# Moving row loads and the stores of the first q from SyncE's DMA queue to GpSimd's in a transformer block

## The chip, the cores and the metric

The kernel runs on one core of one Trainium2 chip. The metric is device time in microseconds (us) for one execution. A run gives several executions of a kernel, with the kernel before run in the same rounds on the same chip.

Engine names are those of the profile: PE is TensorE (matmuls), PEld its weight loads, DVE VectorE, ACT ScalarE, POOL GpSimd, SP SyncE, which here only issues DMAs. SPq is SyncE's sequencer. Of the DMA queues in the profiles, q1 carries what SyncE issues, q0 what GpSimd issues (22.02 MB in the kernel before, the sum of its transfers) and q10 what ScalarE issues. The profile gives the time of each queue's packets as a share of the core's 16 DMA engines; the shares of a stretch can add up to over 100% (108.1% from 16 to 25 us in the kernel before).

## The reference

One transformer block over 2,048 rows of 1,024 numbers in bfloat16: a layer norm, q, k and v products, a dilated attention over 8 positions at distance 2, an output product, a second layer norm, and a gated product with 3,584 columns.

```python
h = x + _A_ref(_layernorm(x, axis=-1), A_wqkv, A_wo)     # qkv, attention, output product
h2 = h + _B_ref(_layernorm(h, axis=-1), B_w_gate, B_w_up, B_w_down)
return h2
```

Only the first layer norm, the qkv product and the loads that attention needs are touched by the change.

## The kernel before

The rows are worked on in four chunks of 512 (c = 0 to 3), each of four tiles of 128 rows (t = 0 to 3). The qkv product wants normalised rows with the 1,024 columns on the partitions. For chunk 0 TensorE turns them itself; for the later ones a DMA transpose does:

```python
def transpose(self, t):                      # Norm1, one row tile of chunk c; line 225
    ...
    nc.sync.dma_start_transpose(lnTs[c][:, :, bass.ts(t, 128)], self.lns[t][:])

def load_x(c, what, eng):                    # four loads of 256 KB; line 198
    tiles = []
    for t in range(4):
        xt = hp.tile([128, D], BF, tag="h", name=f"{what}{c}_{t}")
        eng.dma_start(xt[:], x[bass.ds(c * TC + t * 128, 128), :])
        tiles.append(xt)
    return tiles
```

The product makes six blocks of 512 columns for a chunk (0 and 1 are q, 2 and 3 k, 4 and 5 v), each of four groups m of eight matmuls. ScalarE casts each group, and a DMA stores it to DRAM, from where GpSimd loads it again in the layout that attention wants (qD, kD, vD). The load of q waits until the stores of q have landed.

```python
def evac_qkv(c, m, ps):
    sg = t1k.tile([128, HB + TC], BF, tag="t1k", name=f"sg{c}_{m}")
    nc.scalar.copy(sg[:, HB:HB + TC], ps[:])
    ...
    if m < 8:                                # q: 128 KB, line 297
        nc.sync.dma_start(qd[c][...]...)
        return
    ...                                      # k, v: 144 KB, line 303
    nc.sync.dma_start(dst[...]..., win)

def load_qk(c):
    ...
    nc.gpsimd.dma_start(qD[:], qd[c].rearrange("c g d s -> (c g) d s"))   # 1 MB, line 399
    nc.gpsimd.dma_start(kD[:], kd[c].rearrange("c g d s -> (c g) d s"))
```

The schedule of the first 60 us. `pump(n)` issues the 1 MB weight blocks w1, w2, ... of the product from SyncE. `bg` holds background work (statistics, normalisation, transposes, attention) that is placed between groups of the product.

```python
pump(2, w1)
xtiles[1] = load_x(1, "x", nc.sync)
pump(4)                                      # w2, w3
xtiles[2] = load_x(2, "x", nc.sync)
...
bg.add(rows_gen(norm1[1], True))             # chunk 1: statistics, normalise, transpose
rows2 = rows_gen(norm1[2], False)            # chunk 2: the same, not transposed yet
bg.add(rows2)
...
qkv(0, range(1, 4))                          # chunk 0, blocks 1 to 3
load_qk(0)
bg.finish(rows2)
for t in range(4):
    norm1[2].transpose(t)
xtiles[3] = load_x(3, "x", nc.sync)
...
qkv(1, range(4))                             # chunk 1 needs all four of its transposes
```

Of the kernel before, what the change touches and what calls it, by code (L numbers as in the profile page):

```python
# [23 lines left out]
HB = 16  # L24
TC = 512
# [52 lines left out]
def kernel(  # L78
# [11 lines left out]
    nc = tc.nc  # L90
    x = A_x.flatten_outer_dims()
# [23 lines left out]
    qd = [dram.tile([4, H, DH, SUB], BF, name=f"qd{c}") for c in range(NCH)]  # L115
# [4 lines left out]
    bg = Background()  # L120
# [36 lines left out]
    def pump(limit=None, wt=None):  # L157
        state["limit"] = limit or state["limit"]
        while state["next"] < state["limit"] and state["live"] < 7:
            key, src, n = stream[state["next"]]  # L160
            if wt is None:
                wt = wpool.tile([128, KO, 512], BF, tag="w", name="w_" + "_".join(map(str, key)))
            nc.sync.dma_start(wt[:, 0:n, :], src)
            wts[key] = wt
            wt = None
            state["next"] += 1
            state["live"] += 1

    def retire(n=1):
        state["live"] -= n  # L170
        pump()
# [22 lines left out]
    def load_x(c, what, eng):  # L194
# [6 lines that stand above are left out]
# [3 lines left out]
    xtiles = {}  # L204
# [33 lines left out]
    def stats_gen(n):  # L238
        for t in range(4):
            n.stat(t)  # L240
            yield 1.5
# [46 lines left out]
# [3 lines that stand above are left out]
        hg = m % 8  # L291
        if m >= 8:
            nc.scalar.copy(sg[:, 0:HB], halo[:, m - 8, :])
            if c + 1 < NCH:
                nc.scalar.copy(halo[:, m - 8, :], ps[:, TC - HB:TC])
        if m < 8:
            nc.sync.dma_start(qd[c][:, 4 * hg:4 * hg + 4, :, :].rearrange("c g d s -> (g d) c s"),
                              sg[:, HB:HB + TC].rearrange("p (c s) -> p c s", c=4))
            return
        dst = (kd, vd)[m // 8 - 1][c]  # L300
        base = sg[:, 0:1]
        win = bass.AP(base.tensor, base.offset, [list(base.ap[0]), [SUB, 4], [1, SUB + HB]])
        nc.sync.dma_start(dst[:, 4 * hg:4 * hg + 4, :, :].rearrange("c g d s -> (g d) c s"), win)
# [61 lines left out]
    pump(2, w1)  # L365
    xtiles[1] = load_x(1, "x", nc.sync)
    pump(4)
    xtiles[2] = load_x(2, "x", nc.sync)
    norm1 = {c: Norm1(c) for c in (1, 2, 3)}
    bg.add(rows_gen(norm1[1], True))  # L370
    rows2 = rows_gen(norm1[2], False)
# [1 line left out]
    for j in range(4):  # L373
        evac_qkv(0, j, ps0[j])
    bg.now = 17.0

    def mm_group(ps, wt, j, rhs):
        for ko in range(KO):
            nc.tensor.matmul(ps[:], lhsT=wt[:, ko, bass.ts(j, 128)], rhs=rhs[:, ko, :],  # L379
                             start=(ko == 0), stop=(ko == KO - 1))  # L380

    def qkv(c, blocks, last=False):
        for b in blocks:
            for j in range(4):
                ps = psum.tile([128, TC], F32, tag="mm", name=f"ps{c}_{b}_{j}")
                mm_group(ps, wts["qkv", b], j, lnTs[c])
                evac_qkv(c, b * 4 + j, ps)
                bg.step(GROUP_US)
            if last:
                retire()  # L390
# [5 lines left out]
    def load_qk(c):  # L396
        qD = att.tile([128, DH, SUB], BF, tag="qD", name=f"qD{c}")
        kD = att.tile([128, DH, SUB + HB], BF, tag="kD", name=f"kD{c}")
        nc.gpsimd.dma_start(qD[:], qd[c].rearrange("c g d s -> (c g) d s"))
        nc.gpsimd.dma_start(kD[:], kd[c].rearrange("c g d s -> (c g) d s"))  # L400
        qkv_in["q", c], qkv_in["k", c] = qD, kD
# [250 lines left out]
    def start_attention(c):  # L652
        stored.add(c)
        atts[c] = attention(c)
        bg.add(atts[c], bg.now + (16.0 if c == 0 else 0.0))

    qkv(0, range(1, 4))
    load_qk(0)
    bg.finish(rows2)
    for t in range(4):  # L660
        norm1[2].transpose(t)
    xtiles[3] = load_x(3, "x", nc.sync)
    pump(6)
    bg.add(stats_gen(norm1[3]), bg.now + 6.0)
    start_attention(0)
    qkv(1, range(4))
    qkv(0, range(4, 6))
# [88 lines left out]
```

## Time and profile before

| | before |
|---|---|
| time, median of 3 executions (range) | 809.99 us (809.59 to 810.6) |
| TensorE busy | 794.0 of 808.9 us |
| TensorE waits for chunk 1's transposed rows | 4.3 us |
| granted clock after that pause | 0.51, for 6.0 us |
| chunk 1's product starts at | 42.48 us |

How to read it: TensorE is nearly always busy, so what counts is its few pauses, and the slow clock that a pause may bring (here 0.51 after the pause of 4.3 us). Below, T1 to T4 are the four transposes of chunk 1, in order.

### The profile page before, as it was taken

To read this page: it belongs to the slowest core of one execution; us is meant where nothing else is said; L and a number is where in the kernel's file an instruction comes from. 1 tells how busy PE (TensorE), PEld (TensorE's weight loads), DVE (VectorE), ACT (ScalarE), POOL (GpSimd) and SP (SyncE) were. 2 spreads that over 40 slices of the span, in tenths; PEclk is the share of its full clock that TensorE was granted. 3 is DMA by queue.
4 is the path that set the end of the run, shared out by engine and by line. 5 is a ranking of instruction groups with operands and counts; after the bars stand their busy time and mean duration, and the time that the engine had idled before them with its cause. 6 is when DMAs were issued, how large, how long until landed. Compare 5 with 4: busy or idle time off the path is not lost.

```text
span 808.9 us, 9878 instructions
## 1 busy us (share of the span) xinstructions
PE 794.0 (98%) x3700; PEld 410.3 (51%) x3769; DVE 552.1 (68%) x580; ACT 254.3 (31%) x562; POOL 165.3 (20%) x160
## 2 busy tenths in 40 slices
PE   8889999999999999999999999999999999999998
PEld 5334444444444444444444444466666666644445
DVE  6519999999899998998989926645646556311111
ACT  4516445323333321013333100244555555400000
POOL 0000000200002000010000010597867778000000
PEclk9989999999999999999999999999999999999999
DMA  7998693897956869667637596542313233466500
GB/s 261 249 268 201 167 269 88 265 288 197 330 172 214 286 243 213 213 216 239 202 105 237 172 245 178 130 121 62 104 53 105 68 90 98 158 208 191 179 27 27
DMA packets 195200, 144.32 MB, mean 178 GB/s; under 512 B 83408, under 2 KB 187984, under 8 KB 193104
## 3 DMA queue, kind: packets, MB, share of 16 engines
q1 hardware_dynamic: 191568, 121.66, 53.7%
q0 software_dynamic: 3584, 22.02, 8.3%
q8 instruction: 30, 0.49, 0.3%
q14 instruction: 18, 0.15, 0.1%
HBM read 114.29 MB, written 22.02 MB: 169 GB/s over the span
## 4 chain that ended last, share of the span: by engine, by line
PE 89%; DVE 7%; DMA 2%; issue 1%; ACT 0%; SPq 0%; DVEq 0%
PE ps L379 18%; PE acc L558 15%; PE pg L379 12%; PE pu L379 12%; PE wo L500 7%; PE pz L609 6%; PE py L609 6%; PE px L609 6%; PE pv L609 3%; PE accl L548 3%; DVE pv L462 2%; DMA lnT<-ln 1%; DVE pv L470 1%; PE ps L341 1%; DVE oD L472 1%
## 5 line engine op out<-in xcount | busy, mean ns | idle before, releaser
L379 PE MATMUL ps<-lnT,w_qkv 128*128 128x512 bf16 x721 | 161.3, 383 | 5.2 <-DMA lnT<-ln 4.3
L379 PEld LDWEIGHTS <-w_qkv 128*128 128x128 bf16 x736 | 72.6, 99 | 93.3 <-issue 8.6
L379 PE MATMUL pg<-lnT,w_wg 128*128 128x512 bf16 x439 | 105.0, 379 | 0.5
L379 PE MATMUL pu<-lnT,w_wu 128*128 128x512 bf16 x439 | 104.9, 379 | 0.4
L558 PE MATMUL acc<-w_wd,gs 128*128 128x512 bf16 x439 | 96.7, 379 | 0.5
L540 DVE TENSOR_TENSOR h<-acc,h 128x512 bf16<-128x512 f32 x28 | 17.4, 682 | 91.1 <-PE acc L558 91.1
L290 ACT CAST sg<-ps 128x512 bf16<-128x512 f32 x96 | 55.0, 587 | 68.9 <-PE ps L379 65.4
L462 DVE TENSOR_TENSOR pv<-vD,at 128x4096 bf16<-128x4096 bf16 x32 | 72.5, 2286 | 0.3
L419 DVE TENSOR_TENSOR prod<-qD,kD 128x4096 bf16<-128x4096 bf16 x32 | 72.3, 2283 | 0.1
L379 PEld LDWEIGHTS <-w_wu 128*128 128x128 bf16 x448 | 43.8, 98 | 52.9
L558 PEld LDWEIGHTS <-gs 128*128 128x128 bf16 x448 | 43.8, 98 | 52.9
L379 PEld LDWEIGHTS <-w_wg 128*128 128x128 bf16 x448 | 43.8, 98 | 52.9
L525 ACT CAST gs<-pg 128x512 bf16<-128x512 f32 x56 | 32.9, 588 | 100.0 <-PE pg L379 96.6
L500 PE MATMUL wo<-w_wo,oT 128*128 128x512 bf16 x251 | 55.6, 379 | 0.3
L474 POOL DMA_DIRECT2D od<-oD x4 | 2.2, 542 | 253.1 <-DVE oD L472 253.1
L609 PE MATMUL px<-lnT,w_pair 128*128 128x512 bf16 x210 | 52.5, 380 | 1.0
L585 POOL TENSOR_TENSOR sw<-w_pair 128x512 fp32r<-128x512 bf16 x28 | 36.5, 1304 | 75.6 <-DMA w_pair<-in_B_w_gate_dram 43.3
L530 ACT CAST us<-pu 128x512 bf16<-128x512 f32 x56 | 32.8, 587 | 57.5 <-PE pu L379 54.1
L500 PEld LDWEIGHTS <-oT 128*128 128x128 bf16 x256 | 25.1, 98 | 30.2
L181 ACT ACTIVATE rs<-mv,eps 128x1 f32<-128x1 f32 x32 | 9.5, 296 | 95.5 <-DVE mv L178 91.9
L587 POOL TENSOR_TENSOR sw<-w_pair 128x512 fp32r<-128x512 bf16 x28 | 36.9, 1319 | 0.0
L421 DVE TENSOR_TENSOR prod<-prod 128x4096 bf16<-128x4096 bf16 x16 | 36.6, 2288 | 0.3
(127 smaller groups left out, 1057.9 us busy)
## 6 DMA issues: line engine op xcount, KB each, us to landing
w_wd<-in_B_w_down_dram SPq DMA_DIRECT2D x32, 896.0 KB, 6.3
w_wg<-in_B_w_gate_dram SPq DMA_DIRECT2D x14, 1024.0 KB, 7.1
w_wu<-in_B_w_up_dram SPq DMA_DIRECT2D x14, 1024.0 KB, 5.5
w_wo<-in_A_wo_dram SPq DMA_DIRECT2D x8, 1024.0 KB, 8.0
w_pair<-in_B_w_gate_dram SPq DMA_DIRECT2D x14, 512.0 KB, 4.0
w_pair<-in_B_w_up_dram SPq DMA_DIRECT2D x14, 512.0 KB, 5.3
w_qkv<-in_A_wqkv_dram SPq DMA_DIRECT2D x5, 1024.0 KB, 10.9
kd<-sg SPq DMA_DIRECT2D x32, 144.0 KB, 3.1
```

Of the source, the lines that this page charges most:

```text
L290: nc.scalar.copy(sg[:, HB:HB + TC], ps[:])
L379: nc.tensor.matmul(ps[:], lhsT=wt[:, ko, bass.ts(j, 128)], rhs=rhs[:, ko, :], start=(ko == 0), stop=(ko == KO - 1))
L419: nc.vector.tensor_tensor(prod[:, j], qD[:], kD[:, :, o:o + SUB], ALU.mult)
L421: nc.vector.tensor_tensor(prod[:, :, 0:16], prod[:, :, 0:16], prod[:, :, 16:32], ALU.add)
L462: nc.vector.tensor_tensor(pv[:, j], vD[:, :, o:o + SUB], at[:, w, None, :].to_broadcast((128, DH, SUB)), ALU.mult)
L500: nc.tensor.matmul(ps[:], lhsT=oTs[c][:, kk, t, :], rhs=wts["wo", c, hf][:, kk, :], start=(kk == 0), stop=(kk == KO - 1))
L525: nc.scalar.copy(gs[:], pg[:])
L530: nc.scalar.copy(us[:], pu[:])
L558: nc.tensor.matmul(acc[t][:], lhsT=hT[f][:, bass.ts(t, 128)], rhs=wts["wd", c, hf, b][:, j, :], start=(f == 0), stop=(f == NF - 1))
L585: nc.gpsimd.tensor_tensor(sw[:, 0], a21, a22, ALU.add)
L587: nc.gpsimd.tensor_tensor(sw[:, 2], a11, a21, ALU.subtract)
L609: nc.tensor.matmul(ps[:], lhsT=lhs[:, ko, :], rhs=rhs[:, ko, :], start=(fresh and ko == 0), stop=(ko == 3), skip_group_check=not fresh)
```

## The change

The intent: in the order in which SyncE issues its DMAs, the first transpose of chunk 1 stands behind the four row loads of chunk 2 (5.85 us from 14.62) and six stores of q (7.54 us from 20.57), so it is issued at 28.20. If row loads and q stores go through GpSimd's queue, the transposes are issued earlier, and TensorE should not wait for them.

```diff
@@ evac_qkv
         if m < 8:
-            nc.sync.dma_start(qd[c][...]...)
+            (nc.gpsimd if c == 0 else nc.sync).dma_start(qd[c][...]...)
@@
     pump(4)
-    xtiles[2] = load_x(2, "x", nc.sync)
+    xtiles[2] = load_x(2, "x", nc.gpsimd)
@@
-    qkv(0, range(1, 4))
+    qkv(0, range(1, 2))
+    xtiles[3] = load_x(3, "x", nc.gpsimd)
+    qkv(0, range(2, 4))
     load_qk(0)
     bg.finish(rows2)
     for t in range(4):
         norm1[2].transpose(t)
-    xtiles[3] = load_x(3, "x", nc.sync)
     pump(6)
-    bg.add(stats_gen(norm1[3]), bg.now + 6.0)
+    bg.add(stats_gen(norm1[3]))
```

It has three parts: the rows of chunk 2 on GpSimd's queue ("x2"), the q stores of chunk 0 on it ("q stores"), and the rows of chunk 3 on it and earlier ("x3").

More of the change, by code (lines that the diff above doesn't have):

```diff
@@ L296, in evac_qkv @@
         if m < 8:
-            nc.sync.dma_start(qd[c][:, 4 * hg:4 * hg + 4, :, :].rearrange("c g d s -> (g d) c s"),
-                              sg[:, HB:HB + TC].rearrange("p (c s) -> p c s", c=4))
+            (nc.gpsimd if c == 0 else nc.sync).dma_start(qd[c][:, 4 * hg:4 * hg + 4, :, :].rearrange("c g d s -> (g d) c s"),
+                sg[:, HB:HB + TC].rearrange("p (c s) -> p c s", c=4))
             return
```

## The prediction

The forecast came to 806.5 us: 1.0 us won by an earlier start of chunk 1 and 2.9 us of half clock make 3.9 us, and 3.5 after the chance of one in seven. That the clock stays full in the pauses that are left was the author's estimate, as the trace before has one long pause there (4.3 us, then a clock of 0.51). That three of four x2 tiles go ahead of w1 (the 2.1 us) was an estimate too. The 0.216 us of a matmul is that of the chain of waits (1.73 us for 8). The 1.2 us of a transpose are an estimate: its 256 KB at the 205 GB/s that the kernel before moved from 28 to 34 us would take 1.3 us.

> **What bounds the kernel now.** I read the page first, then TensorE's waits, the chain of waits, stretches around the one long wait, and last the DMA queues there.
>
> ```profile
> PE 794.0 (98%) x3700; PEld 410.3 (51%) x3769; DVE 552.1 (68%) x580; ACT 254.3 (31%) x562; POOL 165.3 (20%) x160
> ...
> PE ps L379 <- DMA lnT<-ln: 4.3, 1, 4.3
> PE warm_ps L284 <- DVE warm L270: 1.2, 1, 1.2
> PE ps L341 <- DMA w_qkv<-in_A_wqkv_dram: 1.1, 1, 1.1
> ```
>
> TensorE is busy for 794.0 of 808.9 us, so all its idle time is 14.9 us. Only one wait is in reach of this change: the 4.3 us in which the qkv product of chunk 1 (line 379) waits for the transposed rows lnT. The other two are start-up, before any instruction that is moved. What that wait costs is more than 4.3 us:
>
> ```profile
> 31.00:38.00 7.00, 7.00 (x34) 3.07 (x32) 4.44 (x9) 3.66 (x15) 0.70 (x1) 1.00 1.16 186
> 38.00:42.40 4.40, 0.22 (x2) 0.00 (x0) 0.04 (x1) 1.13 (x6) 0.00 (x0) 0.90 0.81 259
> 42.40:48.40 6.00, 5.70 (x14) 2.08 (x16) 0.51 (x1) 0.59 (x1) 0.00 (x1) 0.51 1.33 205
> 48.40:54.00 5.60, 5.60 (x28) 2.53 (x27) 0.00 (x0) 1.76 (x3) 0.54 (x1) 1.00 0.98 265
> ```
>
> Columns: stretch, length, busy time (instructions) of TensorE, its weight loads, VectorE, ScalarE and GpSimd, granted clock, DMA share, GB/s. After the pause the granted clock is 0.51 for 6.0 us: 14 matmuls there, against 28 in the 5.6 us after it. At the later rate (0.20 us each by this count; 6.65 us for 30, so 0.22, by the chain below) those 14 would take 3.0 us, so the slow clock costs about 2.9 us. The wait is worth 4.3 + 2.9 = 7.2 us, 0.9% of 810. That is the most the change can win; nothing else on TensorE waits for what it moves.
>
> Why is lnT late? The chain:
>
> ```profile
> 17.77 6.65 PE ps L379 x30
> 28.20 3.17 DMA lnT<-ln
> 34.18 8.05 DMA lnT<-ln
> 42.23 0.25 issue
> 42.48 2.29 PE ps L379 x5
> ```
>
> The first transpose is issued at 28.20 and lands in 3.17 us; the fourth is issued at 34.18 and needs 8.05. So there are two delays: a late issue, and a slow landing. The issue, from the timeline, then the two DMA queues from 36.5 to 41.5 (packets, MB, share of the 16 engines):
>
> ```profile
> 14.62 5.85 SPq L198 DMA_DIRECT2D x<-in_A_x_dram  x4
> 20.57 7.54 SPq L297 DMA_DIRECT2D qd<-sg  x6
> 28.20 1.35 SPq L225 DMA_TRANSPOSE lnT<-ln  x1
> 34.44 0.70 POOL L399 DMA_DIRECT2D qD<-qd  x1 [24.38 <-DMA qd<-sg]
> ...
> q0 software_dynamic: 128, 1.04, 91.5%
> q1 hardware_dynamic: 418, 0.10, 12.3%
> ```
>
> SyncE is held up 5.85 us by the four rows of chunk 2 and 7.54 us by six q stores. The first normalised row was ready at 20.9 (normalisation at 20.37, 0.55 us), so its transpose is 7.3 us late. GpSimd's 1 MB load of q (qD) then starts 0.26 us after the fourth transpose and takes 91.5% of the engines. Alone, that transpose would have landed at 34.18 + 3.2 = 37.4, before TensorE ran dry at 38.2. The collision makes the wait; the late issue makes the collision possible.
>
> [...] From 51 to 54 us [...] 107 packets of q0 beside 87 of q1, but 0.99 MB against 0.02, because GpSimd's packets are 8 to 9 KB and SyncE's 256 B. [...] The DMA share from 16 to 25 us is already 108.1%, all q1: there is none to spare.
>
> **The change part by part.** The instruction order shows that TensorE's and VectorE's orders stay as they are and ScalarE moves three casts; SyncE loses 16 DMAs (4 of x2, 8 of qd, 4 of x3) and GpSimd gains them. Bytes are equal.
>
> Removed: SyncE's 5.85 us and 13 us of stores ahead of transposes. They can be issued at about 21, 23, 25 and 27; the third now stands behind the first k store, which waits for the first product of block 2.
>
> Moved, and now in the way: GpSimd's queue works beside the weights. TensorE needs w1 at 17.28, then, at 32 matmuls of 0.216 us (6.9 us) a block, w2 at 24.2 and w3 at 31.1. In the trace w1, issued at 10.09, lands 5.0 later (15.1), w2 9.3 after 12.69 (22.0), w3 11.9 after 13.17 (25.0). Margins: 2.2, 2.2, 6.1 us.
> - x2: 1 MB at some 360 GB/s (rate of 16 to 25 us) is 2.9 us. Issued from 10.1 on as x0's tiles come free[...]. About three of four tiles precede w1: 15.1 + 2.1 = 17.2. No wait, or 0.5 us.
> - q stores: eight of 128 KB. SyncE's landed 0.45 us apart, taken as the cost of each (estimate). Six have passed by the time w2 lands: 22.0 + 2.9 + 6 x 0.4 = 27.3 against 24.2 needed (24.7 if w1 was late). A new wait of 2.0 to 3.0 us.
> - x3, from about 26: another 2.9 us. w3: 25.0 + 2.9 + 3.2 + 2.9 = 34.0, needed at 27 + 6.9 = 33.9. A wait of 0 to 1 us, longer if qD, now issued near 29, overtakes it.
> - Transposes: behind w3 in the same queue, each about 1.2 us of the engines, sharing with qD's 1 MB: last at 39 to 42. TensorE would finish block 3 at 27 + 13.8 = 40.8. A wait of 0 to 1 us.
>
> Sum: chunk 1 starts near 41.5 instead of 42.48 (1.0 us won), and [...] the 2.9 us of half clock go too: 3.9 us. With a one in seven chance that a pause still trips the clock, 3.5 us. 809.99 - 3.5 = 806.5.
>
> Beside other work: attention of chunk 0 on VectorE may start earlier, as x3's statistics no longer wait 14.3 us for rows loaded at 50.2. Later VectorE waits are not TensorE's waits, so this is worth nothing in the total.
>
> **The rivals.** *A: clean win.* The SyncE queue is what matters, GpSimd's data comes late or trickles, the weights keep their margins, and all 7.2 us go: about 803. For it: transposes could be issued 7 us sooner, and margins of 2.2 us exist. Against it: a DMA share of 108% in that stretch; 1 MB plus stores must displace something[...]. *B: the wait moves to the weights.* w2 waits 3.5 us or more[...], and w3 or the transposes wait again behind x3 and qD: chunk 1 starts at 43 to 46, about 809 to 813. For it: the slow start of qD in the trace (1.04 MB in 5 us, and only 0.10 MB beside it). Against it: w3 has 6 us of margin, and a late block 2 pushes its need back. *C: nothing.* The fourth transpose just meets qD again, both earlier: 809 to 810. My number lies between A and B.
>
> **Range and chances.** The clean win bounds it below at 802.8. Above, a w2 wait of 4 us with cold clock and one more small wait give 811. 802.5 to 811 should hold it 8 times in 10. Two per cent is 16.2 us; the win cannot exceed 7.2, and a loss of 16 would take four waits like the one removed. So within 2% 0.98, faster 0.005, slower 0.015.
>
> **What would show it.** TensorE's waits: no 4.3 us on lnT; instead a wait on w_qkv near 24 us of 2 to 3 us. The granted clock near 1.00 from 38 to 54. First transpose issued near 21 to 22, not 28. The landing of w2 at 11 us or more after its issue, not 9.3; w3 15 or more, not 11.9. Granted clock below 1 after 24 means rival B; no wait over 0.5 us anywhere in 17 to 60 means rival A, and my stores and rows got less of the engines than I gave them. A new wait beyond 60 us, on a row tile or a q, would show that I missed a dependency.

## The result, and the profile after

The kernel after took 820.86 us (median of 4, 820.48 to 822.8), against 809.79 us (808.6 to 810.6) for the kernel before in the same rounds. The ratio is 1.0143, with a 95% interval of 1.0122 to 1.0163. A ratio here is the mean time of one kernel's runs over that of the other's of the same rounds, so it is not quite the ratio of the medians quoted. The change is slower, by less than 2%; the time lies 9.9 us above the predicted range.

First the engines' busy time in the profile of the kernel after (span 819.0 us, before 808.9). TensorE's count shows that all 3,769 matmuls are recorded, while 69 were missing before, so busy times of the two aren't compared; waits and times of day are.

```profile
PE 799.4 (98%) x3769; PEld 410.6 (50%) x3769; DVE 553.3 (68%) x580; ACT 255.5 (31%) x562; POOL 175.5 (21%) x176
```

TensorE's waits after (line, what it waited for: us in total, times, longest):

```profile
PE ps L379 <- DMA lnT<-ln: 11.7, 1, 11.7
PE ps L379 <- DMA w_qkv<-in_A_wqkv_dram: 2.1, 1, 2.1
```

The wait that was to go has grown from 4.3 to 11.7 us, and the new wait for w2 is there with 2.1 us. Now stretches around the two (same columns as in the prediction):

```profile
24.20:26.40 2.20, 0.06 (x2) 0.02 (x2) 1.85 (x5) 0.98 (x3) 1.24 (x2) 0.99 1.04 355
26.40:41.90 15.50, 15.50 (x64) 6.54 (x64) 4.45 (x10) 4.62 (x18) 2.20 (x5) 0.89 1.35 173
41.90:53.60 11.70, 0.12 (x1) 0.00 (x0) 2.49 (x5) 3.53 (x14) 0.00 (x0) 0.71 0.91 131
53.60:57.00 3.40, 3.33 (x8) 1.16 (x9) 3.22 (x7) 0.00 (x0) 0.00 (x0) 0.50 1.38 223
57.00:63.00 6.00, 6.00 (x29) 2.76 (x28) 2.80 (x7) 3.88 (x12) 0.53 (x1) 1.00 1.19 217
```

The clock fell twice: to half for 3.4 us after each pause (the first is inside the second line, whose mean is 0.89 for that reason). In the second stretch the 8 matmuls took 3.33 us; at the 6.00 us for 29 of the line after it they would have taken 1.7 us. So 3.4 us at half clock cost 1.7 us, twice that 3.4 us. So the ledger: after, 2.1 + 11.7 + 3.4 = 17.2 us; before, 4.3 + 2.9 = 7.2 us. The difference of 10.0 us is the difference of the spans (10.1 us), so nothing after 60 us matters.

Why the transposes are late, from the chain of waits after:

```profile
25.34 0.80 DVE ln L186
26.14 0.54 DVE st L177
26.68 26.90 DMA lnT<-ln x2
53.58 0.09 issue
53.67 6.35 PE ps L379 x21
```

and from the timeline of SyncE's and GpSimd's issues (start, length of the group, what, how many; in brackets the idle time before it and what ended it):

```profile
21.36 8.82 SPq L225 DMA_TRANSPOSE lnT<-ln  x2
30.68 0.38 SPq L303 DMA_DIRECT2D kd<-sg  x1
31.16 14.81 SPq L225 DMA_TRANSPOSE lnT<-ln  x2
...
25.90 2.15 POOL L198 DMA_DIRECT2D x<-in_A_x_dram  x4
34.41 0.54 POOL L399 DMA_DIRECT2D qD<-qd  x1 [6.35 <-DMA qd<-sg]
```

The early issue worked for T1, which is issued at 21.36 instead of 28.20. It did not for T4, which is issued at 40.75 instead of 34.18 although its row was ready at 26.1: SyncE needed 9.5 us to issue T3 alone (31.16 to 40.66), where a transpose took it 1.3 us before. And the landing takes the whole gain and more:

| | T1 | T2 | T3 | T4 |
|---|---|---|---|---|
| issued | 21.36 | 26.68 | 31.16 | 40.75 |
| landed | 37.35 | 42.88 | 52.85 | 53.58 |
| us | 16.0 | 16.2 | 21.7 | 12.8 |

Before, T1 landed in 3.17 us. These times run from issue to landing, so they hold what stood ahead in SyncE's own queue: w3 for T1, and the earlier transposes for the others. The weights do not explain the lateness, though: w3 landed at 30.1, and T1 7.2 us after it. From then on only two things are left in flight: transposes (with k stores) in SyncE's queue, and in GpSimd's the last q stores (landed by 33.85), the rows of chunk 3 (landed 35.9 to 40.7), then qD (issued 34.41, landed 52.67). These never leave a gap. The DMA view of 28 to 40 us (packets, MB, rate; then packets, MB and share of the 16 engines of each queue):

```profile
DMA packets 1903, 1.71 MB, mean 143 GB/s; under 512 B 1563, under 2 KB 1583, under 8 KB 1901
...
q0 software_dynamic: 414, 1.31, 70.5%
q1 hardware_dynamic: 1488, 0.39, 31.4%
```

This is the riddle that the experiments are for. The sum of what was to be moved is no more than predicted, but the engines moved it at 143 GB/s, where the prediction had taken some 360 GB/s from the stretch before. They look busy, because packets took long, and carried little: by these shares 0.33 us for one of 3.2 KB in q0 and 0.04 us for one of 0.26 KB in q1, against 0.18 us for 4.3 KB and 0.02 us for 0.27 KB with plain copies in place of the transposes (e8_plain, below).

### The profile page after: what moved, and what is told of

The parts are those of the page before. It is cut to its first block, busy times and chain, and to the rows that moved or that the text cites. A ratio compares the mean times of both kernels' runs of the same rounds, so it can differ in the third digit from the quotient of the medians.

```text
span 819.0 us, 9960 instructions
## 1 busy us (share of the span) xinstructions
PE 799.4 (98%) x3769; PEld 410.6 (50%) x3769; DVE 553.3 (68%) x580; ACT 255.5 (31%) x562; POOL 175.5 (21%) x176
## 4 chain that ended last, share of the span: by engine, by line
PE 95%; DMA 4%; DVE 0%; SPq 0%; ACT 0%; issue 0%
PE acc L558 21%; PE ps L379 18%; PE pg L379 12%; PE pu L379 12%; PE wo L500 7%; PE pz L609 6%; PE py L609 6%; PE px L609 6%; DMA lnT<-ln 3%; PE pv L609 3%; PE accl L548 3%; PE ps L341 1%; DMA w_qkv<-in_A_wqkv_dram 1%; PE pt L331 0%; SPq L257 0%; DVE ln L186 0%
## 5 line engine op out<-in xcount | busy, mean ns | idle before, releaser
L379 PE MATMUL ps<-lnT,w_qkv 128*128 128x512 bf16 x736 | 162.8, 384 | 13.8 <-DMA lnT<-ln 11.7
L609 PE MATMUL px<-lnT,w_pair 128*128 128x512 bf16 x224 | 55.6, 381 | 0.0
## 6 DMA issues: line engine op xcount, KB each, us to landing
w_qkv<-in_A_wqkv_dram SPq DMA_DIRECT2D x5, 1024.0 KB, 12.8
```

The source lines that it names most:

```text
L379: nc.tensor.matmul(ps[:], lhsT=wt[:, ko, bass.ts(j, 128)], rhs=rhs[:, ko, :], start=(ko == 0), stop=(ko == KO - 1))
L609: nc.tensor.matmul(ps[:], lhsT=lhs[:, ko, :], rhs=rhs[:, ko, :], start=(fresh and ko == 0), stop=(ko == 3), skip_group_check=not fresh)
```

## The experiments

Two theories to start with. **Bytes**: the engines carry so many bytes a microsecond (362 GB/s was measured from 16 to 25 us in the kernel before) whatever is in flight, and what is late is late because of what is ahead of it. **Collision**: transposes in flight beside another queue's transfers slow both down, beyond their bytes. The first set tries the parts one by one, the second asks what is needed for the slowing, the third builds on what was learned, and the last tries to give it a size. Times are medians. `n` is the number of runs of the kernel tried.

| kernel | time, us | before, same rounds | ratio (95%) | n |
|---|---|---|---|---|
| e1_x2_only | 813.18 | 810.56 | 1.0044 (1.0014 to 1.0075) | 4 |
| e2_qd_only | 806.32 | 810.56 | 0.9954 (0.9922 to 0.9985) | 4 |
| e3_x3_only | 813.29 | 810.56 | 1.0039 (1.0013 to 1.0065) | 4 |
| e4_without_x3 | 807.00 | 810.56 | 0.9960 (0.9929 to 0.9992) | 4 |
| e5_before_gate | 809.89 | 810.27 | 1.0003 (0.9982 to 1.0023) | 6 |
| e6_gate_q | 810.50 | 810.27 | 1.0010 (0.9987 to 1.0033) | 4 |
| e7_act_gate_q | 810.03 | 810.27 | 1.0007 (0.9982 to 1.0032) | 4 |
| e8_plain (wrong) | 806.87 | 810.27 | 0.9963 (0.9930 to 0.9997) | 2 |
| e9_qd_gate | 809.55 | 808.99 | 1.0004 (0.9985 to 1.0023) | 4 |
| b1_gate_rows_first | 803.06 | 808.99 | 0.9928 (0.9913 to 0.9942) | 6 |
| b2_qd_gate_rows_first | 804.58 | 808.99 | 0.9941 (0.9920 to 0.9961) | 6 |
| e10_dose | 804.32 | 808.99 | 0.9945 (0.9927 to 0.9964) | 4 |
| e11_rows_sync | 807.33 | 808.11 | 0.9985 (0.9956 to 1.0013) | 4 |
| e12_dose_four | 808.10 | 808.11 | 0.9996 (0.9972 to 1.0021) | 4 |
| e13_early_loads | 809.12 | 808.76 | 1.0005 (0.9984 to 1.0027) | 2 |
| e14_early_stores | 811.32 | 808.76 | 1.0033 (1.0012 to 1.0053) | 2 |
| e15_last_stores_sync | 807.98 | 808.76 | 0.9996 (0.9979 to 1.0014) | 4 |

All but e8_plain gave right results. The trace is of one execution: that of e1_x2_only is the slowest of its four (815.83 us), that of b2_qd_gate_rows_first the slowest of its six (807.03 us). Where two kernels of different rounds are set side by side below, their ratios to the kernel before are what is compared.

### The parts one by one

**e1_x2_only**: the kernel before with the first part alone.

```diff
-    xtiles[2] = load_x(2, "x", nc.sync)
+    xtiles[2] = load_x(2, "x", nc.gpsimd)
```

> Only the rows of chunk 2 go to GpSimd's queue. Theory 'bytes' (that of the prediction: the engines stay full, [...] every moved byte costs its time once): w2 lands 2.9 us later, at about 25, so a wait of 0.7 us on w_qkv; the transposes are issued 2 us earlier and land no later than before, so the wait on lnT shrinks to 2 us or less: 804 to 808. Theory 'collision' (a transpose in flight beside packets of GpSimd's queue slows both far below what the engines can move): the rows have landed before the first transpose moves data, so only the load of q collides, as before: wait on lnT 3 to 5 us, 808 to 811.

Measured: 813.18 us, slower than either theory had it. T4 was issued at 34.66 and landed at 48.03 (13.4 us), beside T3 and qD. TensorE stood still up to 48.1 for that (a pause of 9.3 us, which the profile puts down to issue) and ran at half clock for 5.3 us after it. Why T4 took 13.4 us here and 8.05 us in the kernel before is not shown: in both, T3 was issued over 1 us and T4 0.3 us before qD. The execution traced is also 2.6 us slower than the median, so the usual pause was shorter.

**e2_qd_only**: the second part alone.

```diff
-            nc.sync.dma_start(qd[c][...]...)
+            (nc.gpsimd if c == 0 else nc.sync).dma_start(qd[c][...]...)
```

> Only the eight q stores of chunk 0 go to GpSimd's queue. Theory 'bytes': the transposes are issued from about 21 us on, behind w3 and the rows of chunk 2, and land by 37: no wait on lnT, 803 to 806. Theory 'collision': the last q stores and then the load of q, which now starts near 29 to 31, lie on all four transposes: wait on lnT of 4 to 8 us, 810 to 816, and under 150 GB/s while both are in flight.

Measured: 806.32 us, a gain. T4 went from 32.93 to 40.30, and TensorE waited 1.9 us for it with the clock full (mean 1.000 in the traced execution). The part is good by itself, and better than collision had it; bytes had no wait at all.

**e3_x3_only**: the third part alone.

```diff
-    qkv(0, range(1, 4))
+    qkv(0, range(1, 2))
+    xtiles[3] = load_x(3, "x", nc.gpsimd)
+    qkv(0, range(2, 4))
...
-    xtiles[3] = load_x(3, "x", nc.sync)
```

> Only the rows of chunk 3 go to GpSimd's queue, early. Theory 'bytes': 1 MB more before the fourth transpose, 2.9 us: wait on lnT 7 us, 812 to 814. Theory 'collision': rows from about 27 us on and then the load of q lie on all transposes: wait on lnT of 8 us or more, 814 to 821, and under 150 GB/s while both are in flight.

Measured: 813.29 us, with a wait of 7.7 us on lnT: near the number of bytes. It does not test collision with the rows, though: the rows landed from 28.5 to 31.4, and T1, issued at 29.99, landed 3.9 us later, so it hardly met them. T4 went from 36.47 to 45.41 beside qD: it landed 3.2 us later than before, and 2.3 us of that is its later issue.

**e4_without_x3**: the change without the third part, so x2 and the q stores together.

```diff
 # against the kernel after
-    qkv(0, range(1, 2))
-    xtiles[3] = load_x(3, "x", nc.gpsimd)
-    qkv(0, range(2, 4))
+    qkv(0, range(1, 4))
...
+    xtiles[3] = load_x(3, "x", nc.sync)
```

> The changed kernel with the rows of chunk 3 back at their old place on SyncE's queue. Theory 'bytes': 2.9 us less than the changed kernel, 818, with the engines full from 27 to 50 us. Theory 'collision': the first transpose meets only the last q stores and the others the load of q, four tiles fewer to collide with: wait on lnT falls from 11.7 to 4 to 8 us, 811 to 816.

Measured: 807.00 us. Both theories missed, on the slow side. Without x3 the other two parts win: no wait on lnT is left, only the one for w2 (2.1 us, then half clock for 3.4 us). So without x3 there is no loss; x3 with only one of the other two was not tried. The parts do not add up either: alone they change the time by +0.44, -0.46 and +0.39%, together by +1.43%. The DMA view shows what differs, for 28 to 33 us, where both queues had work, and for 33 to 36 us, where GpSimd's was empty:

```profile
DMA packets 1370, 0.61 MB, mean 121 GB/s; under 512 B 1283, under 2 KB 1307, under 8 KB 1369
...
DMA packets 3019, 0.77 MB, mean 256 GB/s; under 512 B 3019, under 2 KB 3019, under 8 KB 3019
```

While q stores were in flight in the other queue, the packets under 512 B, of both queues, came at 1,283 in 5 us (257 a us); once it was empty, those of SyncE's alone came at 3,019 in 3 us (1,006 a us). T1, issued at 21.44, landed at 33.48, right at the end of the stores; the rest followed fast, T4 at 40.42 even beside qD. The kernel after has no such gap because its x3 rows and then qD follow the stores without a pause.

### What the slowing needs

**e6_gate_q**: the change, but with qD held back until T4 has landed. A tiny copy on GpSimd reads transposed rows into qD before the load, so the load must wait for it. The load then overwrites the values, and the result stays right.

```diff
 # load_qk, against the kernel after
+        if c == 0:
+            nc.gpsimd.tensor_copy(qD[:, 0, 0:4],
+                lnTs[1].rearrange("p k (t s) -> p k t s", t=4)[:, 0, :, 0])
         nc.gpsimd.dma_start(qD[:], qd[c]...)
```

> The changed kernel with the same copy: the load of q starts after all four transposes, the rows of chunk 3 still lie on them. If the load of q makes most of the 11.7 us wait: no or under 3 us of wait on lnT, 806 to 811. If the rows of chunk 3 make most of it: transposes 2 to 4 still take over 10 us each, wait 7 us or more, 815 to 821.

Measured: 810.50 us. T1 still took from 21.25 to 38.05, beside the stores and rows. The last of the rows landed at 40.7; T2 followed at 41.23, T3 at 43.06 and T4, issued at 40.66, at 43.94, in 3.3 us. Set beside the kernel after (1.0143 - 1.0010, times 810), about 11 us of the loss need qD behind the rows; T1's lateness does not need qD.

**e7_act_gate_q**: the same with the x3 rows issued from ScalarE's queue instead.

```diff
 # against e6_gate_q
-    xtiles[3] = load_x(3, "x", nc.gpsimd)
+    xtiles[3] = load_x(3, "x", nc.scalar)
```

> As the run before, but the rows of chunk 3 go from ScalarE's queue, a second hardware queue, instead of GpSimd's. If the collision belongs to the software queue: transposes beside them take their share and no more, DMA over 250 GB/s from 28 to 36 us, wait on lnT under 1 us, 805 to 808. If any second queue does it: as the run before, within 2 us.

Measured: 810.03 us; T1 took from 21.53 to 39.59, and the core moved 134 GB/s from 28 to 38 us: 0.82 MB through ScalarE's queue (q10) and 0.26 MB, the last q stores, through GpSimd's. The transposes were as late as in e6_gate_q, so moving the rows to ScalarE's queue does not help. But it does not clear GpSimd's queue: its last store landed only at 38.02, so it too had work beside T1 nearly to the end. From 38 to 40 us, with only ScalarE's rows beside the transposes, the core moved 215 GB/s. Whether a queue of ScalarE's alone slows transposes is not shown.

**e8_plain**: the kernel after, where chunk 1's transposes are replaced by plain copies of the same bytes in pieces of 256 B, into the same tiles. The result is wrong (relative error 0.71), so only its times count.

```diff
 # Norm1.transpose, against the kernel after
-            nc.sync.dma_start_transpose(lnTs[c][:, :, bass.ts(t, 128)], self.lns[t][:])
+            if c == 1:
+                nc.sync.dma_start(lnTs[c][:, :, bass.ts(t, 128)], self.lns[t].rearrange("p (k s) -> p k s", k=KO))
+            else:
+                nc.sync.dma_start_transpose(...)
```

> The changed kernel with the four transposes of chunk 1 made plain copies of the same bytes in pieces of 256 B, from the same queue at the same place; the result is wrong on purpose. If the collision needs transposes: the engines stay over 200 GB/s from 28 us on, no wait on lnT above 2 us, 806 to 810. If any small packets beside GpSimd's queue do it: wait on lnT of 8 us or more, 816 to 821.

Measured: 806.87 us, no wait on lnT at all; the copies landed between 33.5 and 39.4, each 8.2 to 12.5 us after its issue. From 28 to 40 us:

```profile
DMA packets 6263, 3.78 MB, mean 315 GB/s; under 512 B 5823, under 2 KB 5843, under 8 KB 6133
...
q1 hardware_dynamic: 5735, 1.52, 58.3%
q0 software_dynamic: 526, 2.24, 49.1%
```

Same queues, same issue order, 256 B packets again, and both queues move: 315 GB/s against the 143 of the kernel after. So neither the small packets nor the bytes are the cause. It needs transposes.

**e11_rows_sync**: the kernel after, with the x3 rows at the same early place but through SyncE's queue, which the transposes use too.

```diff
 # against the kernel after
-    xtiles[3] = load_x(3, "x", nc.gpsimd)
+    xtiles[3] = load_x(3, "x", nc.sync)
```

> The changed kernel with the rows of chunk 3 at the same early place, but from SyncE's queue, where the transposes are: same bytes, same time, one queue. If it is the second queue that hurts: the first transpose lands near 33.5 as without the rows, over 200 GB/s while rows and transposes move, and only the load of q meets the last two transposes: wait on lnT 2 to 6 us, 808 to 814. If early rows hurt from any queue: wait of 10 us or more, 819 to 822.

Measured: 807.33 us (ratio 0.9985, against 1.0143 for the kernel after). The rows landed at 35.2 to 37.4, T1 at 33.91, T2 at 34.52, T3 at 39.95, T4 at 42.82, beside qD; no wait on lnT beyond 0.3 us. From 33 to 38 us, with rows and transposes in one queue:

```profile
DMA packets 2494, 1.54 MB, mean 309 GB/s; under 512 B 1982, under 2 KB 1982, under 8 KB 2494
...
q1 hardware_dynamic: 2494, 1.54, 103.7%
```

The same bytes at the same place of the program, and one queue in place of two: this is the cleanest of the pairs. With the queue the order changes too: the rows now stand behind T1 and T2 and are issued at 30.28 to 31.90, 4.4 us later than in the kernel after. They are still ahead of T3 and T4, so bytes is ruled out as the explanation of the 11.7 us; it needs the rows in another queue than the transposes.

**e15_last_stores_sync**: the kernel after with the last three q stores back on SyncE, meant to make a gap in GpSimd's queue.

```diff
-            (nc.gpsimd if c == 0 else nc.sync).dma_start(qd[c][...]...)
+            (nc.gpsimd if c == 0 and m < 5 else nc.sync).dma_start(qd[c][...]...)
```

> The changed kernel with the last three q stores of chunk 0 back on SyncE's queue, so that only the rows of chunk 3 and then the load of q meet the transposes. If the stores start the slowing: wait on lnT under 4 us, 806 to 812. If the rows and the load of q are enough: wait of 8 us or more, 817 to 821.

Measured: 807.98 us, with no wait on lnT beyond 0.3 us. It is not a pure test, because the order of things moved: two of the x3 rows landed early (27.1 and 28.8), and qD was issued only at 39.25. But it has the same step in it as e4_without_x3. From 34 to 37 us the last two rows (36.2 to 36.8) were in flight beside T1, which took from 22.48 to 37.09; from 37 to 40 us nothing of GpSimd's queue moved:

```profile
DMA packets 683, 0.21 MB, mean 72 GB/s; under 512 B 671, under 2 KB 671, under 8 KB 683
...
DMA packets 3099, 0.79 MB, mean 262 GB/s; under 512 B 3099, under 2 KB 3099, under 8 KB 3099
```

### Is the wait of the kernel before the same thing?

**e5_before_gate**: the kernel before with the gate on qD.

```diff
 # load_qk
+        if c == 0:
+            nc.gpsimd.tensor_copy(qD[:, 0, 0:4],
+                lnTs[1].rearrange("p k (t s) -> p k t s", t=4)[:, 0, :, 0])
```

> The kernel before, with one small copy on GpSimd that reads the transposed rows, so that the load of q starts only after the fourth transpose has landed. Theory 'collision' (the load of q is what made the fourth transpose take 8.05 us): it lands 3.2 us after its issue at 34.2, about 37.4, before TensorE needs it at 38.2; no wait on lnT, clock stays full: 7.2 us less, 802 to 804. Theory 'late issue' (SyncE's queue alone makes it late): the wait stays at 3 to 4 us, 808 to 810.

Measured: 809.89 us, nothing won. Yet the gate did its work: T4 took from 34.47 to 37.72 (3.25 us in place of 8.05), and the wait on lnT is gone. The waits from 40 to 66 us show what came for it:

```profile
DVE st L177 <- DMA x<-in_A_x_dram: 19.8, 1, 19.8
ACT rs L181 <- DVE mv L178: 16.0, 4, 13.8
...
PE ps L379 <- ACT sg L290: 4.5, 1, 4.5
```

To be read from the bottom: TensorE waits 4.5 us for ScalarE to empty a bank (sg). ScalarE stood in its own order behind the statistics of chunk 3 for 13.8 us, and VectorE, which makes them, waited 19.8 us for the rows of chunk 3. Those are behind chunk 2's transposes in SyncE's queue, of which the last took 9.5 us. They landed at 60.26, only 1.0 us later than before; what is new is that TensorE, without its old pause, gets there sooner. A new bound had lain right behind the old one.

**e9_qd_gate**: the same with the q stores on GpSimd's queue (the edit of e2_qd_only).

> The kernel before with the q stores of chunk 0 on GpSimd's queue and the load of q behind the transposes; the rows of chunk 3 stay at their old place. Against the q stores alone (1.9 us of wait at 38 us): that wait goes, but if the rows of chunk 3 then bound the start of chunk 1's second half, as in the gated kernel before, 1 to 4 us come back near 58 us: 804 to 809, about where the q stores alone were.

Measured: 809.55 us. T4 landed at 35.39, and TensorE waited 3.7 us for ScalarE from 58.6 on instead, as expected: an earlier T4 is worth nothing while that wait stands.

### A version that beats both

**b1_gate_rows_first**: the gate, and the rows of chunk 3 issued ahead of chunk 2's transposes, all on SyncE as before.

```diff
 # against e5_before_gate
     bg.finish(rows2)
+    xtiles[3] = load_x(3, "x", nc.sync)
     for t in range(4):
         norm1[2].transpose(t)
-    xtiles[3] = load_x(3, "x", nc.sync)
```

> The gate on the load of q alone won nothing: the fourth transpose landed at 37.7, but TensorE then waited 4.5 us at 58.7 for ScalarE, which waited 13.8 us for the statistics of chunk 3, whose rows stood behind the transposes of chunk 2. Here those rows are issued ahead of these transposes, still from SyncE. If that is the whole of it: no wait over 0.5 us after start-up, clock full: 7 us less than before, 802.5 to 804. If the rows' place was not the cause, a wait of 4 us stays: 808 to 810.

Measured: 803.06 us (802.81 to 803.76), ratio 0.9928. Its busy times, and all of TensorE's waits in the profile:

```profile
PE 792.1 (99%) x3700; PEld 409.8 (51%) x3769; DVE 552.4 (69%) x580; ACT 254.3 (32%) x562; POOL 165.6 (21%) x161
...
PE warm_ps L284 <- DVE warm L270: 1.2, 1, 1.2
PE ps L341 <- ACT lnT L333: 0.5, 1, 0.5
```

Only start-up is left. 808.99 - 803.06 = 5.9 us is most of the 7.2 us that the prediction gave as the most that could be won here. Part of the gap may be the clock: the kernel before does not pay the half clock in every execution, as three of the eleven in these rounds show a mean clock of 1.000. b1_gate_rows_first has no part of the change in it.

**b2_qd_gate_rows_first**: b1_gate_rows_first with the q stores on GpSimd's queue.

> The same, with the q stores of chunk 0 on GpSimd's queue as in the change. If the stores only help by getting the transposes out earlier, nothing is left to win: equal to the run before, 802.5 to 804. If stores in flight beside the first transpose delay it, 0 to 3 us of wait on lnT: 803 to 807.

Measured: 804.58 us (802.48 to 807.03), not clearly different from b1_gate_rows_first, as the intervals overlap. T4 landed at 35.81 instead of 36.98. In the traced execution, the slowest of the six, a new wait of 2.5 us on a weight block appeared at 65.9 us, since a transpose of chunk 2 took from 45.75 to 63.10 beside kD: a collision again, one chunk on. Three of the six took 802.5 to 803.6 us, so it is not in every execution.

### How large is the slowing?

Four kernels on the clean base of b1_gate_rows_first, each with idle transfers from GpSimd's queue (they go to or from a tile that nothing reads), started at a chosen time by a small copy that reads what must have landed.

**e10_dose**: one load of 256 KB after T2 has landed.

```diff
 # load_qk, c == 0, ahead of the gate
+            nc.gpsimd.tensor_copy(probe[:, 0:1], lnTs[1][:, 0, 128:129])
+            nc.gpsimd.dma_start(probe[:], x[0:128, :])
```

> As the first of this batch, with one load of 256 KB from GpSimd's queue, into a tile that nothing reads, started when the second transpose has landed (about 34 us), so that it lies on the last two. 'bytes': 256 KB at 360 GB/s is 0.7 us: the last transpose lands by 38.5, wait on lnT under 0.6 us, 803 to 804.5. 'collision': it lands at 39.5 or later, wait on lnT 1.5 to 5 us, 804.5 to 810.

Measured: 804.32 us; T4 took from 34.36 to 38.86, TensorE waited 0.9 us. Between the theories: inconclusive.

**e12_dose_four**: four such loads from about 31.6 us on, so beside T3 and T4.

```diff
+            nc.gpsimd.tensor_copy(probe[:, :, 0:1], lnTs[1][:, 0:4, 0:1])
+            for t in range(4):
+                nc.gpsimd.dma_start(probe[:, t, :], x[bass.ds(t * 128, 128), :])
```

> The best kernel so far with four loads of 256 KB from GpSimd's queue into a tile that nothing reads, started when the first transpose has landed (about 31.5 us), so that their data lie on the last two transposes. Bytes alone: 1 MB at 360 GB/s is 2.9 us, the last transpose lands by 40.5, wait on lnT 2.3 us or less, 803 to 806. If the slowing grows with what lies on the transposes: it lands at 42 or later, wait 4 us or more with a cold clock after it, 809 to 815.

Measured: 808.10 us. T4 landed at 40.50, 3.5 us later than in b1_gate_rows_first; the bytes alone (1 MB at 360 GB/s) are 2.9 us. From 33 to 39 us the core moved 268 GB/s with both queues at work. So a second queue does not always slow transposes much. The time missed what bytes had (803 to 806 us) all the same. And in the same execution a transpose of chunk 2 took 15.6 us (44.45 to 60.09) beside kD.

**e13_early_loads**: the same four loads from 27.5 us, so beside T1 too.

```diff
+    nc.gpsimd.tensor_copy(probe[:, :, 0:1], norm1[2].mv4[:, 0:1, 0:1].to_broadcast((128, 4, 1)))
+    for t in range(4):
+        nc.gpsimd.dma_start(probe[:, t, :], x[bass.ds(t * 128, 128), :])
```

> The best kernel with four idle loads of 256 KB from GpSimd's queue again, but started at about 27.5 us, so that they lie on the first transposes with two or more to come. Bytes: 1 MB is 2.9 us, the last transpose lands at 40 or a little later as with the later dose (40.5), wait on lnT 2 to 3 us, 806 to 809. If it matters that several transposes stand in the queue: it lands at 43 or later, wait 5 us or more, 810 to 816.

Measured: 809.12 us. T1 took from 27.83 to 35.79, T4 landed at 41.33: 4.3 us later, against 2.9 by bytes. In between.

**e14_early_stores**: eight stores of 128 KB in the q layout in their place.

```diff
+    for t in range(8):
+        nc.gpsimd.dma_start(pd[t][:, 0:4, :, :].rearrange("c g d s -> (g d) c s"), probe[...]...)
```

> The same place, with eight idle stores of 128 KB in pieces of 256 B, as the q stores are, instead of the loads. Bytes: 3.6 us at 0.45 each, the last transpose lands by 41, wait 3 us, 807 to 809. If stores on the second queue are what slows the transposes: it lands at 43 or later, 810 to 818, and under 150 GB/s from 29 us on.

Measured: 811.32 us. T4 landed at 43.80; less some 0.9 us that this execution was late from the start (an odd start-up wait on a row), that is about 5.9 us later, against some 3.6 us for eight stores at the 0.45 us that the prediction took for one. From 29 to 44 us the core moved 186 GB/s, more than the 150 that the expectation gave as a sign. In these two traces stores delayed T4 more than loads did; with two timed executions of each, and the late start, that is a hint and no more.

## Why the prediction was wrong

It expected a gain of 3.5 us, within 2% either way, and got a loss of 11. The direction was wrong, the range was missed, and that the change lies within 2% was right.

**What held.** T1 issued "at about 21": 21.36. "A new wait of 2.0 to 3.0 us" on w2: 2.1 us. No wait on w1: none. "w3 15 or more" after its issue: 17.2 us (12.97 to 30.1), though the absolute 34.0 was too late, because the x3 rows did not come in ahead of it. TensorE ended block 3 of chunk 0 near 41.9 where the prediction has 40.8, and 1.7 us of that is the slow clock. No new wait beyond 60 us, and earlier attention worth nothing: right. Up to 41.9 us the forecast of TensorE's progress is good to about a microsecond.

Some of that is luck. On w1 the reason was wrong: three x2 tiles were to land ahead of it, but it landed at 14.98, before all four (16.51 to 21.14). On w2 the prediction's own sum, 27.3 against 24.2 or 24.7, gives 2.6 to 3.1 us; four stores had landed before w2 (26.34), not six. "21, 23, 25 and 27" for the issues held for T1 alone (then 26.68, 31.16 and 40.75). Of the readings, "all its idle time is 14.9 us" is not right, since 69 matmuls are missing from that trace; the waits it lists add up to 7.8 us. The timeline has 8.6 us of q stores ahead of transposes (six in 7.54 us, then 0.52 and 0.53), not 13. How the two queues share the engines differs between its two views: 107 packets of q0 beside 87 of q1 in one, 128 beside 418 in the other.

**The step that failed** is this one: "Transposes: behind w3 in the same queue, each about 1.2 us of the engines, sharing with qD's 1 MB: last at 39 to 42", with "A wait of 0 to 1 us". T4 landed at 53.58, and the wait was 11.7 us. The step costs every transfer by its bytes, from "Bytes are equal" on. That bookkeeping is right for plain transfers: the plain copies of e8_plain landed by 39.4. It is wrong for transposes in flight beside another queue. Shown: plain copies in place of transposes take the loss away (e8_plain), the same rows in the transposes' own queue take it away (e11_rows_sync), and in a gap of the other queue the transposes move fast (e4_without_x3, e15_last_stores_sync). The change moved three transfers so that GpSimd's queue was never empty from before T1's issue until 52.67 us: stores, then rows, then qD. Taking any one link out brought the time to between 807 and 811 us (e4_without_x3, e6_gate_q, e11_rows_sync, e15_last_stores_sync).

The evidence was in the prediction itself. Its profile has the fourth transpose at 8.05 us beside qD, against 3.17 us alone, and it says "The collision makes the wait". It then priced the new collisions as a sum of bytes, although the change moved 3 MB more into the colliding queue. The price was some 360 GB/s, the rate from 16 to 25 us at a DMA share of 108.1%; in the kernel after, from 28 to 40 us, shares of 70.5 and 31.4% went with 143 GB/s. Rival C ("The fourth transpose just meets qD again") named the right pair, and rival B ("the transposes wait again behind x3 and qD") came nearest, with its sign, a clock below 1 after 24 us; but B had chunk 1 start at 43 to 46, and it started at 53.67. Neither let the wait grow. That a loss of 16 us "would take four waits like the one removed" kept every wait at 4.3 us as well; here one alone took 11.7.

**A second, smaller failure** is the clock. The prediction let "the 2.9 us of half clock go too", with "a one in seven chance that a pause still trips the clock". The clock halved after the 2.1 us pause at 24.2. Of the traces with a pause of 2.0 to 2.2 us there, those of e4_without_x3, e6_gate_q, e11_rows_sync and e15_last_stores_sync show the same; in e7_act_gate_q pauses of 2.1 and 2.9 us, and in e8_plain one of 2.1, left it full (granted clock 1.00 after each). It differs between executions of one kernel, too: the mean clock of e4_without_x3 is 0.998 in the traced one and 1.000 in its other three. One in seven was too low a chance for a pause of this length. It made 1.7 us of the loss, and the second fall, after 11.7 us, another 1.7. How long a pause must be to halve the clock is not shown.

**The size of the whole.** The most to be won, "7.2 us", was well put: b1_gate_rows_first won 5.9 us. The prediction's claim that "nothing else on TensorE waits for what it moves" was true only as long as this wait was there: in e5_before_gate TensorE waited for the rows of chunk 3.

**What stays open.** What in the engines makes a transpose slow beside another queue isn't settled; no run looks inside them. Nor is its size: e12_dose_four lost about what the bytes cost (3.5 us against 2.9), e13_early_loads 4.3 us against 2.9, e14_early_stores some 5.9 against 3.6, and in e11_rows_sync T4 beside qD took 7.8 us where e1_x2_only had 13.4 (3.25 in e5_before_gate, with qD held back). A second queue with work is needed in these runs, but it isn't enough by itself for a large slowing. Whether that queue must be GpSimd's is open as well, since GpSimd's queue had work beside T1 in e7_act_gate_q too. That a longer backlog of transposes makes it worse, and stores more than loads, fits some of the runs and is not shown.

## What to carry to other kernels

Before a transfer is moved to another queue to free the issuer, ask what it will then be in flight beside: a shared queue had kept the transposes of this kernel apart from the rows and stores, and that was worth more than the earlier issue (T1 was issued 6.8 us sooner, and T4 landed at 53.58 instead of 42.23). Where DMA transposes are on the path that sets the end, try to have no other queue's work beside them, as T4 took 8.05 us beside qD and 3.25 us with qD held back (the kernel before and e5_before_gate). Issue the rest in their queue ahead of or behind them (the rows of chunk 3 so: ratio 0.9985 in e11_rows_sync, against 1.0143), or hold it with a small copy that reads what they wrote. And when a wait is removed and the time stays, read the waits again, for the next one may have been right behind it, as the rows of chunk 3 were (4.5 us in e5_before_gate).
